# Attention and hash-routed experts on one core: transposes a pair ahead of the scores, row-table sums behind the outputs, warm-up ahead of the routing sums

## The chip, the cores and the metric

The kernel runs on one core of one Trainium2 chip. Its time is device microseconds, the median of three runs; the profile is one further execution of the same program. PE is TensorE (PEld its weight loads), DVE VectorE, ACT ScalarE, POOL GpSimd, SP SyncE.

## The reference

Two stages are joined. The first is causal attention in blocks of 64 over 8 sequences of 576 positions, 8 heads of 64. The second sends every one of the 4608 resulting rows to one of 8 experts, chosen by a hash of its token id, and applies two matrix products with a ReLU between them.

```python
scores = scale * np.matmul(q, k.transpose(0, 1, 3, 2))     # B, H, S, D = 8, 8, 576, 64
scores = np.where(block_i >= block_j, scores, -1000000000.0)
attn = softmax(scores)
x = np.matmul(attn, v)                                      # to rows of 512: N = B * S = 4608
...
expert_idx = token_ids * np.int64(2654435761) % np.int64(E) # E = 8
out[mask] = np.maximum(x[mask] @ w1[e], 0.0) @ w2[e]        # D = 512, F = 1024
```

## The kernel before

Everything is placed by hand: every engine runs its instructions in the order in which the program writes them, and only semaphores order the engines among themselves. A place in the program text is therefore a place in five queues.

**Attention.** The work is cut into 32 pairs of heads, `g` = 0 to 31, four pairs for each sequence `b`. The main loop has one turn for each pair, and a last turn, g = 32, for what is left. In a turn:

- `S_chunk(g, 0)` and `S_chunk(g, 1)`: PE makes two of three chunks of scores (L172, with the mask matmuls at L182) into a PSUM tile `ps` of pool `psS` (two buffers). ACT takes the exponential of each into `pt` (L200).
- In some turns `place_b`: five matmuls on PE (L412) that add a share of the row table, and a DVE addition into `acc` (L415). They use the last 144 columns of the first bank of the tile `O` (pool `psO`, one buffer), which `place_b` allocates; `PV` of the same turn then uses the tile's first 325 columns.
- `PV(g - 1, m)`: the outputs of the pair before (L237, L242), into `O`.
- `norm(g - 1)`: DVE divides by the row sums and writes `xs` (L254, L255).
- `S_chunk(g, 2)`: the third chunk, and at the first pair of a sequence `S_rest`, the last 64 positions (L208, L213).
- `T_group(b, n)`: one of four groups of 18 transposes of a later sequence (L159) into `tp` (pool `psT`, one buffer), which DVE copies to `qT` or `kT` (L164). Groups 2 and 3 are the keys, 0 and 1 the queries. Before the change sequence b's four groups lie in turns 4b-4 to 4b-1, and its scores begin in turn 4b.
- `steps`: pieces of the routing. `route` is a generator that computes, for every token, its slot among the experts; its scan (L304) and the count sums on PE (L318, L319) belong to turn 0. `place_a` makes one-hot tables on DVE (L387, L391), `place_p` multiplies them on POOL (L398, L401), and `place_b` sums them, four turns after `place_a`. The turns of `place_b` are 9, 11, ... 23 (`mids`). `placed` turns the sums into the row table `perm3` in turn 24.
- `write_x`: once a sequence is finished, its rows go to `x_dram` (L263, L265), on SP's queue for sequences 0 to 4, on POOL's for 5 to 7.
- `loads`: POOL issues the inputs of later sequences (`load_qk` L107, `load_v` L124 and L127) and the first experts' weights (`load_w1` L449, `load_w2` L454). Inputs are cast from float32 to bfloat16 on the way.
- `gather_x(e, t0, t1)`: indirect reads of rows of `x_dram` for an expert (L461). The first three blocks of experts 0 and 1 need only sequences 0 to 5, and are issued in turns 26 and 27.

Ahead of the loop come the constants, the first part of `route` (five small matmuls at L286 which wait for the token ids on DVE), the loads of sequences 0 and 1, 40 matmuls on a tile of ones (`warm`, L478), and the four transpose groups of sequence 0, whose copies are shared between DVE and ACT.

**Experts.** After the loop POOL gathers the remaining rows. For each expert PE transposes the gathered rows (L553), DVE copies them to `xT` (L554), PE makes the hidden layer (L566, L585), ACT the ReLU (L571, L589), PE the output (L599), DVE copies it (L604) and POOL scatters it to the result (L606). The tiles `xT` lie where attention's buffers were.

Of the kernel before, what the change touches and what calls it, by code (L numbers as in the profile page):

```python
# [10 lines left out]
F32 = mybir.dt.float32  # L11
# [20 lines left out]
GA = EARLY // 128  # L32
OVT = 32
NG = E * G + OVT
WARM = 40
# [5 lines left out]
def kernel(  # L41
# [10 lines left out]
    nc = tc.nc  # L52
    P = nc.NUM_PARTITIONS
# [13 lines left out]
    onesbf = const.tile([P, P], BF16, name="onesbf")  # L67
# [4 lines left out]
    ov_i = const.tile([1, OVT + 1], I32, name="ov_i")  # L72
    inc = const.tile([P, E], F32, name="inc")

    nc.gpsimd.iota(jmp[:], pattern=[[1, P]], base=0, channel_multiplier=-1,
                   allow_small_or_imprecise_dtypes=True)
    nc.vector.tensor_single_scalar(identbf[:], jmp[:], 0.0, op=ALU.is_equal)
    nc.vector.tensor_single_scalar(lower[:], jmp[:], 0.0, op=ALU.is_gt)
    nc.vector.memset(onesbf[:], 1.0)

    nc.vector.memset(maskk[:], 0.0)
    nc.vector.memset(maskq[:], 0.0)
# [5 lines left out]
    psS = att_ctx.enter_context(tc.tile_pool(name="psS", bufs=2, space=bass.MemoryType.PSUM))  # L88
    psT = att_ctx.enter_context(tc.tile_pool(name="psT", bufs=1, space=bass.MemoryType.PSUM))
    psO = att_ctx.enter_context(tc.tile_pool(name="psO", bufs=1, space=bass.MemoryType.PSUM))  # L90
# [30 lines left out]
    def load_v(b):  # L121
        vx, v4 = vexts[b % NV]
        for i in range(NT):
            nc.gpsimd.dma_start(  # L124
                vx[:, :, i, 0:D], v[b, :, 128 * i : 128 * i + 128, :].rearrange("h p d -> p h d"))
        for m in range(2):
            nc.gpsimd.dma_start(  # L127
                v4[64 * m : 64 * m + 64, :, m, 0:D],
                v[b, 4 * m : 4 * m + 4, 512:576, :].rearrange("r s d -> s r d"))
# [20 lines left out]
    def T_group(b, n, pool=None):  # L150
        if b not in qkTs:
            qkTs[b] = [att.tile([P, NP, S], BF16, name=x, tag=x, bufs=3) for x in ("qT", "kT")]
        w, z = divmod(n, 2)
        c0, n = RUN // 2 * z, RUN // 2
        pool, tag = pool or (psT, "tp")
        tp = pool.tile([P, 16, P], BF16, name="tp", tag=tag)
        for c in range(n):
            for m in range(2):
                nc.tensor.transpose(out=tp[64 * m : 64 * m + 64, c, :],  # L159
                                    in_=loaded[b][w][:, m, c0 + c, :], identity=identbf[:])  # L160
        parts = ((nc.vector.tensor_copy, 0, P),) if b > 0 else (
            (nc.vector.tensor_copy, 0, 64), (nc.scalar.copy, 64, P))
        for copy, r0, r1 in parts:
            copy(qkTs[b][w][:].rearrange("p r (j c) -> p (r j) c", c=RUN)[:, r0:r1, c0 : c0 + n],  # L164
                 tp[:, 0:n, r0:r1].rearrange("p c r -> p r c"))
# [25 lines left out]
    def S_chunk(g, ch):  # L191
        b, pr = divmod(g, NP)
        ps = psS.tile([P, 2, 512], F32, name="ps", tag="ps")
        for n, (o0, kt, q0, w) in enumerate(CHUNKS[ch]):
            mm_pair(b, pr, ps, o0, kt, q0, w, first=n == 0)
        for o0 in MASKS[ch]:
            mm_mask(ps, o0, last=o0 == MASKS[ch][-1])
        pt = pts[g % 2]
        ptv = pt[:, 0 : 2 * PTW].rearrange("p (m n) -> p m n", m=2)
        nc.scalar.activation(ptv[:, :, 512 * ch : 512 * ch + 512], ps[:], ACT.Exp, scale=SCALE)  # L200
# [24 lines left out]
    ots = {}  # L225

    def PV(g, m):
        b, pr = divmod(g, NP)
        h = pr + NP * m
        pt = pts[g % 2]  # L230
        vx, v4 = vexts[b % NV]
        if g not in ots:
            ots[g] = psO.tile([P, 2, 512], F32, name="O", tag="O")
        O = ots[g][:, m, 0 : 5 * (D + 1)].rearrange("p (t d) -> p t d", t=5)
        for t in range(5):
            for n, (o0, i) in enumerate(PVS[t]):
                nc.tensor.matmul(  # L237
                    O[:, t, :], lhsT=pt[:, m * PTW + o0 : m * PTW + o0 + 128], rhs=vx[:, h, i, 0 : D + 1],
                    start=(n == 0), stop=(n == t),
                )  # L240
            if t == 4:
                nc.tensor.matmul(  # L242
                    O[:, t, :], lhsT=pt4s[b % 2][:, pr * 64 : pr * 64 + 128],
                    rhs=v4[:, pr, m, 0 : D + 1], start=False, stop=True,
                )

    def norm(g):
        b, pr = divmod(g, NP)
        if b not in xss:
            xss[b] = xfix[b % 3]  # L250
        xs = xss[b]
        O = ots.pop(g)[:, :, 0 : 5 * (D + 1)].rearrange("p m (t d) -> p m t d", t=5)
        rs = att.tile([P, 2, 5, 1], F32, name="rs", tag="rs")
        nc.vector.reciprocal(rs[:], O[:, :, :, D : D + 1])  # L254
        nc.vector.tensor_tensor(  # L255
            out=xs[:].rearrange("p t (m r d) -> p r m t d", m=2, r=NP)[:, pr],
            in0=O[:, :, :, 0:D], in1=rs[:].to_broadcast([P, 2, 5, D]), op=ALU.mult,
        )

    def write_x(b):  # L260
        xs = xss[b]
        eng = nc.sync if b < BA - 1 else nc.gpsimd
        eng.dma_start(  # L263
            x_dram[S * b : S * b + 512, :].rearrange("(t p) d -> p t d", p=P), xs[:, 0:NT, :])
        eng.dma_start(x_dram[S * b + 512 : S * b + S, :], xs[0:64, NT, :])  # L265
# [139 lines left out]

    def place_b(b, g):
        ohp, ohg, _ = places.pop(b)
        ots[g] = psO.tile([P, 2, 512], F32, name="O", tag="O")
        pq = ots[g][:, 0, 512 - 2 * NG :]
        for i in range(5):  # L410
            n = P if i < NT else 64
            nc.tensor.matmul(pq, lhsT=ohp[0:n, i, :],  # L412
                             rhs=ohg[0:n, i, :, :].rearrange("p w g -> p (w g)"),
                             start=(i == 0), stop=(i == 4))
        nc.vector.tensor_tensor(out=acc[:].rearrange("p w g -> p (w g)"),  # L415
                                in0=acc[:].rearrange("p w g -> p (w g)"), in1=pq, op=ALU.add)

# [39 lines left out]
    def gather_x(e, t0=0, t1=G):  # L457
        n = N if t1 > GA else BA * S
        for t in range(t0, t1):
            g = e * G + t  # L460
            nc.gpsimd.indirect_dma_start(  # L461
                out=xgs[g % (2 * G)][:], out_offset=None, in_=x_dram[0:n, :],
                in_offset=bass.IndirectOffsetOnAxis(ap=perm3[:, g : g + 1], axis=0),
                bounds_check=n - 1, oob_is_err=False,
            )


    NPAIRS = B * NP
    nc.sync.dma_start(tid[:], moe_token_ids.rearrange("(b s) -> b s", b=B))
    rgen = route()  # L470
    next(rgen)
    load_qk(0)
    load_v(0)
    load_qk(1)
    load_v(1)
    warm = psS.tile([P, 2, 512], F32, name="warm", tag="ps")
    for n in range(WARM):
        nc.tensor.matmul(warm[:, 0, 0:P], lhsT=onesbf[:], rhs=onesbf[:], start=True, stop=True)  # L478
    T_group(0, 2)
    T_group(0, 3, pool=(psO, "O"))  # L480
    T_group(0, 0, pool=(psS, "ps"))
    T_group(0, 1, pool=(psS, "ps"))

    Ts = {g: [] for g in range(NPAIRS + 1)}
    for b in range(1, B):
        for z, n in enumerate((2, 3, 0, 1)):
            Ts[4 * b - 4 + z].append((b, n))
    steps = {g: [] for g in range(NPAIRS + 1)}
    steps[0] += [lambda: next(rgen), lambda: next(rgen)]
    steps[1].append(lambda: next(rgen))  # L490
# [2 lines left out]
    mids = {}  # L493
# [3 lines left out]
        mids[9 + 2 * j] = j  # L497
    steps[24].append(placed)
    loads = {g: [] for g in range(NPAIRS + 1)}
    for b, at in ((2, 0), (3, 4), (4, 7), (5, 10), (6, 13), (7, 16)):  # L500
        loads[at].append((load_qk, b))
        loads[at + 1].append((load_v, b))
    for g, what in ((19, (load_w1, 0)), (20, (load_w1, 1)), (24, (load_w2, 0)), (27, (load_w2, 1))):
        loads[g].append(what)
    for g in range(NPAIRS + 1):
        b, pr = divmod(g, NP)
        live = g < NPAIRS
        if live:
            S_chunk(g, 0)
            S_chunk(g, 1)  # L510
        if g in mids:
            place_b(mids[g], g - 1)
        if g >= 1:
            PV(g - 1, 0)
            PV(g - 1, 1)
            norm(g - 1)
        if live:
            S_chunk(g, 2)
            if pr == 0:
                S_rest(b)  # L520
        for bn in Ts[g]:
            T_group(*bn)
        for step in steps[g]:
            step()
        if pr == 0 and b >= 1:
            write_x(b - 1)
        if 12 <= g < 12 + 2 * G:
            nc.gpsimd.memset(xgs[g - 12][:], 0.0)
        if g in (26, 27):
            gather_x(g - 26, 0, GA)  # L530
        for load, n in loads[g]:
            load(n)
    att_ctx.close()
# [115 lines left out]
    with tc.For_i(0, n_ov, 1) as j:  # L649
# [21 lines left out]
        for ft in range(NFT):  # L671
            hp = psY.tile([P, P], F32, name="hpo", tag="yp")
            for db in range(NKT):
                nc.tensor.matmul(hp[:], lhsT=w1b[:, db, ft::NFT], rhs=xt[:, db, :],
                                 start=(db == 0), stop=(db == NKT - 1))
            nc.scalar.activation(ht[:, ft, :], hp[:], ACT.Relu)
        yp = psY.tile([P, DM], F32, name="ypo", tag="yp")
        for ft in range(NFT):
            nc.tensor.matmul(yp[:], lhsT=ht[:, ft, :], rhs=w2b[:, ft, :],
                             start=(ft == 0), stop=(ft == NFT - 1))  # L680
# [36 lines left out]
```

The softmax here doesn't subtract the row's maximum and nothing guards it: scores larger than these inputs give would overflow.

## Time and profile before

| | |
|---|---|
| time, median of three runs | 337.07 us (336.7 to 337.87) |
| span of the profiled execution | 337.6 us |
| PE busy | 263.3 us (78%) |
| POOL busy | 167.9 us (50%) |
| ACT busy | 143.3 us (42%) |
| DVE busy | 138.5 us (41%) |
| first scores (L172) | 14.8 us |
| last `xs` of attention (L255) ends | 149.05 us |
| last scatter (L606) starts | 327.70 us |
| DMA moved | 50.36 MB, 149 GB/s over the span |

Shares of the whole span mix two stages. Attention ends at 149 us, the experts take the rest; what the change does must be read from the first stage and from the hand-over to the second. An engine's idle time counts only where the others wait for it at that moment, so the waits and the order of events at one place matter more than the sums.

### The profile page before, as it was taken

Reading aid. Unit: us, or ns where it says so; the run is one execution under the profiler, and the core shown is the slowest. Engines: PE = TensorE matmul, PEld = TensorE weight load, DVE = VectorE, ACT = ScalarE, POOL = GpSimd, SP = SyncE. Lnnn points to the kernel's source line nnn. Section 1 sums busy time; section 2 is a strip of 40 time slices with the busy share of each in tenths; the row PEclk is TensorE's granted clock in tenths of the full one; section 3 lists DMA queues with packets and bytes.
Section 4 is the critical chain, followed back from the end, with each engine's and each line's share of the span. In section 5 each row is a group of like instructions: output and inputs, shape, how many; then the busy total and the mean of one; then the engine's idle time right before and its main releaser. Section 6 shows DMA issues by size and latency. Waiting matters only on the chain. (4 is left out here: it accounts for less than half of the span.)

```text
span 337.6 us, 7650 instructions
## 1 busy us (share of the span) xinstructions
PE 263.3 (78%) x3255; PEld 195.2 (58%) x3255; DVE 138.5 (41%) x263; ACT 143.3 (42%) x173; POOL 167.9 (50%) x217
## 2 busy tenths in 40 slices
PE   1749768786878765747789899799798897999970
PEld 1637656575756654535576594675666746668430
DVE  6347696777777544321111414033132140330430
ACT  1437768686868655832252060330320503314000
POOL 8838937949950252116237507437257174050550
PEclk9958999999999995896799999999799999999996
DMA  7999699999999098212109979677766786337330
GB/s 104 181 185 171 109 196 227 136 207 186 190 190 228 34 213 165 80 62 59 47 19 209 188 191 221 176 141 220 160 108 229 139 217 179 66 140 127 128 132 12
DMA packets 53571, 50.36 MB, mean 149 GB/s; under 512 B 40098, under 2 KB 44004, under 8 KB 51488
## 3 DMA queue, kind: packets, MB, share of 16 engines
q0 software_dynamic: 50480, 46.87, 78.2%
q1 hardware_dynamic: 3056, 2.99, 2.9%
q8 instruction: 26, 0.43, 0.5%
q14 instruction: 9, 0.07, 0.1%
HBM read 67.15 MB, written 15.20 MB: 244 GB/s over the span
## 5 line engine op out<-in xcount | busy, mean ns | idle before, releaser
L200 ACT ACTIVATE pt<-ps 128x1024 bf16<-128x1024 f32 x96 | 92.6, 1026 | 36.8 <-PE ps L182 33.0
L571 ACT ACTIVATE hT<-hp 128x640 bf16<-128x640 f32 x48 | 33.3, 703 | 95.3 <-PE hp L566 82.5
L599 PE MATMUL yp<-w2b,hT 128*128 128x512 bf16 x320 | 70.2, 379 | 0.0
L566 PE MATMUL hp<-xT,w1b 128*128 128x320 bf16 x384 | 56.2, 304 | 9.0 <-ACT hT L571 6.7
L566 PEld LDWEIGHTS <-w1b 128*128 128x128 bf16 x384 | 52.6, 145 | 12.6 <-issue 10.4
L606 POOL DMA_INDIRECT out_dram<-ysb,perm x40 | 39.8, 994 | 38.8 <-DVE ysb L604 32.2
L461 POOL DMA_INDIRECT xg<-x_dram,perm x40 | 40.5, 1013 | 26.7 <-issue 14.1
L172 PE MATMUL ps<-qT,kT 64*128 64x512 bf16 (+4 forms) x320 | 37.2, 307 | 20.5 <-DVE qT L164 10.2
L599 PEld LDWEIGHTS <-hT 128*128 128x128 bf16 x320 | 31.1, 98 | 36.1
L604 DVE COPY ysb<-yp 128x512 f32<-128x512 f32 x40 | 27.7, 692 | 55.9 <-PE yp L599 47.7
L554 DVE COPY xT<-tpx 128x512 bf16<-128x512 bf16 x40 | 15.5, 420 | 74.2 <-PE tpx L553 68.3
L237 PE MATMUL O<-vx,pt 128*128 128x65 bf16 x896 | 36.1, 197 | 7.8 <-DVE acc L415 3.9
L237 PEld LDWEIGHTS <-pt 128*128 128x128 bf16 x896 | 32.4, 100 | 10.2 <-issue 7.1
L172 PEld LDWEIGHTS <-kT 64*128 64x128 bf16 x320 | 13.3, 95 | 31.3 <-DVE qT L164 12.9
L124 POOL DMA_DIRECT2D vx<-in_v_dram x32 | 28.6, 914 | 0.3 <-issue 0.2
L255 DVE TENSOR_TENSOR xs<-O,rs 128x640 bf16<-128x640 f32 x32 | 26.4, 824 | 1.1
L164 DVE COPY kT<-tp 128x1152 bf16<-128x1152 bf16 (+1 forms) x16 | 20.4, 1283 | 13.5 <-PE tp L159 13.5
L585 PE MATMUL hp<-xT,w1b 128*128 128x384 bf16 (+1 forms) x128 | 21.1, 329 | 3.2 <-DVE xT L554 3.2
L449 POOL DMA_DIRECT2D w1b<-in_moe_w_dram x8 | 4.7, 589 | 35.3 <-PE tpx L553 35.3
L164 DVE COPY qT<-tp 128x1152 bf16<-128x1152 bf16 (+1 forms) x16 | 20.4, 1280 | 3.3 <-PE ps L182 2.6
L589 ACT ACTIVATE hT<-hp 128x768 bf16<-128x768 f32 (+1 forms) x16 | 11.3, 704 | 23.4 <-PE hp L585 11.0
L553 PE MATMUL tpx<-identbf,xg 128*128 128x128 bf16 x160 | 13.7, 220 | 9.1 <-DVE xT L554 7.8
(107 smaller groups left out, 241.3 us busy)
## 6 DMA issues: line engine op xcount, KB each, us to landing
w1b<-in_moe_w_dram POOLq DMA_DIRECT2D x8, 1024.0 KB
w2b<-in_moe_w_dram POOLq DMA_DIRECT2D x8, 1024.0 KB
vx<-in_v_dram POOLq DMA_DIRECT2D x32, 128.0 KB
kb<-in_k_dram POOLq DMA_DIRECT2D x7, 576.0 KB
qb<-in_q_dram POOLq DMA_DIRECT2D x7, 576.0 KB
x_dram<-xs SPq DMA_DIRECT2D x5, 512.0 KB, 8.1
x_dram<-xs POOLq DMA_DIRECT2D x3, 512.0 KB
xg<-x_dram,perm POOLq DMA_INDIRECT x40
```

What stands on the lines that cost most here:

```text
L124: nc.gpsimd.dma_start(vx[:, :, i, 0:D], v[b, :, 128 * i : 128 * i + 128, :].rearrange("h p d -> p h d"))
L164: copy(qkTs[b][w][:].rearrange("p r (j c) -> p (r j) c", c=RUN)[:, r0:r1, c0 : c0 + n], tp[:, 0:n, r0:r1].rearrange("p c r -> p r c"))
L172: nc.tensor.matmul(ps[:, m, o0 : o0 + n], lhsT=kT[rows, pr, 128 * kt : 128 * kt + 128], rhs=qT[rows, pr, q0 : q0 + n], start=first, stop=F ...
L200: nc.scalar.activation(ptv[:, :, 512 * ch : 512 * ch + 512], ps[:], ACT.Exp, scale=SCALE)
L237: nc.tensor.matmul(O[:, t, :], lhsT=pt[:, m * PTW + o0 : m * PTW + o0 + 128], rhs=vx[:, h, i, 0 : D + 1], start=(n == 0), stop=(n == t),)
L255: nc.vector.tensor_tensor(out=xs[:].rearrange("p t (m r d) -> p r m t d", m=2, r=NP)[:, pr], in0=O[:, :, :, 0:D], in1=rs[:].to_broadcast([ ...
L461: nc.gpsimd.indirect_dma_start(out=xgs[g % (2 * G)][:], out_offset=None, in_=x_dram[0:n, :], in_offset=bass.IndirectOffsetOnAxis(ap=perm3[ ...
L566: nc.tensor.matmul(hp[:, t, 0:HC], lhsT=w1b[:, db, ft::NFT], rhs=xT[:, db, t * HC : (t + 1) * HC], start=(db == 0), stop=(db == NKT - 1),)
L571: nc.scalar.activation(hT[:, ft, :].rearrange("p (t n) -> p t n", t=2), hp[:, :, 0:HC], ACT.Relu)
L599: nc.tensor.matmul(yp[:], lhsT=hT[:, ft, tt * P : (tt + 1) * P], rhs=w2b[:, ft, :], start=(ft == 0), stop=(ft == NFT - 1),)
L604: nc.vector.tensor_copy(ysb[:], yp[:])
L606: ins = nc.gpsimd.indirect_dma_start(out=out[:, :], out_offset=bass.IndirectOffsetOnAxis(ap=perm3[:, gg : gg + 1], axis=0), in_=ysb[:], in ...
```

## The change

It has five parts, all in attention.

1. The transposes of a sequence end a pair of heads before its first scores. A turn now has two places for them: place 0 after the second chunk of scores, ahead of `PV`, and place 1 where they were. Sequence 1 has turns 1, 2, 2, 3, sequence 2 has 4, 5, 6, 6, and later sequences 4b-5 to 4b-2.
2. `place_b` comes after `PV` and uses the tile `O` of that `PV`; its addition into `acc` becomes `place_c` and follows `norm` on DVE.
3. The ones are set first of all on DVE, and the warm-up matmuls stand ahead of the routing's first matmuls on PE.
4. Inputs of sequence 2 are issued in turns 1 and 3 instead of 0 and 1; w1 of expert 1 in turn 21 instead of 20, w2 of expert 0 in 22 instead of 24, w2 of expert 1 in 29 instead of 27.
5. The early gathers are issued in turns 28 and 29 instead of 26 and 27.

```diff
+    nc.vector.memset(onesbf[:], 1.0)
     nc.gpsimd.iota(jmp[:], ...)
...
-    nc.vector.memset(onesbf[:], 1.0)
...
     def place_b(b, g):
         ohp, ohg, _ = places.pop(b)
-        ots[g] = psO.tile([P, 2, 512], F32, name="O", tag="O")
         pq = ots[g][:, 0, 512 - 2 * NG :]
...
+        return pq
+
+    def place_c(pq):
         nc.vector.tensor_tensor(out=acc[:].rearrange("p w g -> p (w g)"), ...)
...
+    warm = psS.tile([P, 2, 512], F32, name="warm", tag="ps")
+    for n in range(WARM):
+        nc.tensor.matmul(warm[:, 0, 0:P], lhsT=onesbf[:], rhs=onesbf[:], start=True, stop=True)
     rgen = route()
     next(rgen)
     load_qk(0)
     load_v(0)
     load_qk(1)
     load_v(1)
-    warm = psS.tile([P, 2, 512], F32, name="warm", tag="ps")
-    for n in range(WARM):
-        nc.tensor.matmul(...)
...
-    Ts = {g: [] for g in range(NPAIRS + 1)}
+    Ts = {(g, z): [] for g in range(NPAIRS + 1) for z in range(2)}
     for b in range(1, B):
-        for z, n in enumerate((2, 3, 0, 1)):
-            Ts[4 * b - 4 + z].append((b, n))
+        at = {1: ((1, 1), (2, 0), (2, 1), (3, 0)), 2: ((4, 1), (5, 1), (6, 0), (6, 1))}.get(
+            b, tuple((4 * b - 5 + z, 1) for z in range(4)))
+        for n, gz in zip((2, 3, 0, 1), at):
+            Ts[gz].append((b, n))
...
-    for b, at in ((2, 0), (3, 4), (4, 7), (5, 10), (6, 13), (7, 16)):
-        loads[at].append((load_qk, b))
-        loads[at + 1].append((load_v, b))
-    for g, what in ((19, (load_w1, 0)), (20, (load_w1, 1)), (24, (load_w2, 0)), (27, (load_w2, 1))):
+    for b, g in enumerate((1, 4, 7, 10, 13, 16), 2):
+        loads[g].append((load_qk, b))
+        loads[g + 1 if b > 2 else 3].append((load_v, b))
+    for g, what in ((19, (load_w1, 0)), (21, (load_w1, 1)), (22, (load_w2, 0)), (29, (load_w2, 1))):
...
-        if g in mids:
-            place_b(mids[g], g - 1)
+        for bn in Ts[g, 0]:
+            T_group(*bn)
         if g >= 1:
             PV(g - 1, 0)
             PV(g - 1, 1)
+            if g in mids:
+                pq = place_b(mids[g], g - 1)
             norm(g - 1)
+            if g in mids:
+                place_c(pq)
...
-        for bn in Ts[g]:
+        for bn in Ts[g, 1]:
             T_group(*bn)
...
-        if g in (26, 27):
-            gather_x(g - 26, 0, GA)
+        if g in (28, 29):
+            gather_x(g - 28, 0, GA)
```

More of the change, by code (lines that the diff above doesn't have):

```diff
@@ L475 @@
     load_v(1)
-    warm = psS.tile([P, 2, 512], F32, name="warm", tag="ps")
-    for n in range(WARM):
-        nc.tensor.matmul(warm[:, 0, 0:P], lhsT=onesbf[:], rhs=onesbf[:], start=True, stop=True)
     T_group(0, 2)
```

## The prediction

> **What bounds the kernel now.** I read the page first, then the waits of PE, then busy time by stage, then the timeline of two places. The chain of waits is of no use here: it ends after two pieces, 1.1 us long.
>
> The page's head and slices (each digit is tenths of a slice of 8.44 us):
> ```profile
> span 337.6 us, 7650 instructions
> ...
> PE   1749768786878765747789899799798897999970
> ...
> DVE  6347696777777544321111414033132140330430
> ACT  1437768686868655832252060330320503314000
> ...
> PEclk9958999999999995896799999999799999999996
> DMA  7999699999999098212109979677766786337330
> ```
> The reader sees two halves. Up to about 149 us (17 slices, attention) PE, DVE and ACT are all at 6 to 8 tenths and DMA at 9: four engines nearly balanced, none full, so the time is set by hand-overs. After that PE alone is near full; the diff touches nothing there. Two dips of the clock (slices 3 and 4; 15 to 18) lie in attention.
>
> Who PE waits for (us in total, times, longest):
> ```profile
> PE ps L172 <- DVE qT L164: 10.2, 7, 1.5
> ...
> PE O L237 <- DVE acc L415: 3.9, 8, 0.6
> ...
> PE pb L318 <- DVE cnt L316: 3.0, 1, 3.0
> PE ps L172 <- issue: 2.4, 1, 2.4
> ```
> The first line is one wait of 1.46 us at each of seven sequence starts: the scores need the last transposes, whose copy (L164) is still running. The second is the row-table sum: PV (L237) waits until the sum (L415) has left the same PSUM tile.
>
> One such sequence start in the timeline (start, length, idle before):
> ```profile
> 64.42 1.36 DVE L164 COPY qT<-tp 128x1152 bf16<-128x1152 bf16 x1
> 65.69 0.81 DVE L387 TENSOR_TENSOR ohp<-iota_p,slo 128x640 bf16<-128x640 bf16 x1
> ...
> 65.83 0.39 PE L172 MATMUL ps<-qT,kT 64*128 64x512 bf16 x2 [1.46 <-DVE qT L164]
> ...
> 66.36 2.86 ACT L200 ACTIVATE pt<-ps 128x1024 bf16<-128x1024 f32 x3 [1.48 <-PE ps L182]
> ```
> PE and ACT stand still together, so this wait is on the path. The start of the kernel:
> ```profile
> 18.49 1.17 PE L159 MATMUL tp<-identbf,kb 128*64 128x128 bf16 x18 [0.86 <-DMA kb<-in_k_dram]
> ...
> 19.70 1.36 DVE L164 COPY kT<-tp 128x1152 bf16<-128x1152 bf16 x1 [5.02 <-PE tp L159]
> ...
> 22.69 0.20 PE L318 MATMUL pb<-cnt,lower 128*128 128x16 bf16 x1 [3.04 <-DVE cnt L316]
> ...
> 22.85 0.61 PE L172 MATMUL ps<-qT,kT 64*128 64x512 bf16 x2
> ...
> 23.55 1.94 ACT L200 ACTIVATE pt<-ps 128x1024 bf16<-128x1024 f32 x2 [5.11 <-PE ps L182]
> ```
> PE waits for the second sequence's keys, DVE copies their transposes, only then runs the routing scan, and PE waits for that: ACT is idle 5.11 us, and matmuls afterwards take 0.61 us instead of 0.39.
>
> Busy time of a sequence and of two odd stretches (PE, PEld, DVE, ACT, POOL, clock, DMA, GB/s):
> ```profile
> 49.80:65.80 16.00, 12.46 (x282) 9.93 (x282) 12.17 (x19) 11.86 (x13) 12.28 (x16) 1.00 1.30 181
> ...
> 122.30:132.80 10.50, 4.65 (x70) 3.07 (x66) 4.81 (x6) 4.04 (x4) 5.46 (x6) 0.71 0.78 177
> ...
> 149.10:154.70 5.60, 1.19 (x12) 0.99 (x13) 1.18 (x3) 0.00 (x0) 2.38 (x3) 0.63 0.27 107
> ```
> A sequence takes 16.0 us, and no engine has over 12.5 us of work in it.
>
> [...]a clock of 0.50 around 18 to 27 us after PE's idling, 0.61 against 0.39 us. [...]PV writes columns 0 to 324, the sum reads 368 to 511, and PV still waited 8 times.[...]
>
> **The change part by part.** Start-to-start steps, warm, read off the timeline of pairs without waits (pair 24 on PE: scores 0 at 113.08, PV at 113.68, scores 2 at 114.69, end 115.07): first two scores 0.60, PV 1.01, third score 0.38, transposes 0.64, row-table matmuls 0.52 (L412, 101.52 to 102.04). DVE: norm 1.00 (0.26 + 0.74), copy of transposes 1.27 (64.42 to 65.69), one-hots of place_a 1.18 (58.42 to 59.60), sum 0.30. ACT: 0.92 to 0.98 per exponential, 0.41 for S_rest.
>
> *Warm-up first, the ones set first.* The 40 matmuls (4.0 us) now run at 7.26 to 11.26 and hold the first transposes back until 11.19; they move to about 1.5 to 5.5 us, while PE has nothing to do. Then the transposes follow the inputs. The last half of q has landed by 11.5 us (GpSimd waits for it until 11.54). From there 0.69 (warm) to 1.17 us (cold) of transposes and 0.8 of copy: scores start at 13.0 to 13.5 instead of 14.82. I take 13.5[...]. That cold clock stays through pairs 0 and 1, as it does now for pair 1.
>
> *Transposes of sequence 1 after pair 1 instead of pair 0.* The scan now runs straight after the first copies (2.6 us of DVE from about 13.4), so PE finds the counts ready, and pair 1 starts when ACT frees a buffer: about 17.2 instead of 22.85. Pairs 1 to 3 then hold four transposes and copies through one PSUM buffer: copy 1.27 + transposes 0.65 + gap each, with two norms between. Adding these up pair by pair: pair 2 at 21.6, pair 3 at 25.8, pair 4 when the last copy ends, 29.4 against 34.89. So -5.5. Moving loads of sequence 2 to pairs 1 and 3 is hidden: the queue is busy with sequence 1 until about 24 us, and they are needed from pair 4 on.
>
> *Pairs 4 to 7* hold the four transposes of sequence 2 in three pairs plus one of sequence 3, the last routing steps (1.9 of DVE) and two place_a (2.36). DVE: 4 norms 4.0 + 5 copies 6.4 + 1.9 + 2.4 = 14.7 us, the engine that sets the pace, against 14.96 measured from pair 4 to 8; with two waits for the single transpose buffer I get the norm of pair 7 at 47.4 against 51.57. So the gain falls to -4.2 here.
>
> *Sequences 2 to 4 (pairs 8 to 19).* The boundary wait (1.46) goes: copies end a pair ahead. The row-table wait (0.4 to 0.58, two a sequence) goes from PE; the sum queues on DVE behind the norm, and ahead of the copy, which is 0.3 later. The norm itself must now wait for the five row-table matmuls[...]: +0.52. The new cycle of two pairs is: norm 1.00, sum 0.30, copy 1.27, one-hots 1.18, norm 1.00, PV 1.01 (it needs that norm: one O buffer), row-table matmuls 0.52, about 0.2 of latencies: 6.5 us, 12.9 a sequence. PE (5.8 for two pairs) and ACT (5.5 to 6.3) fit beside it. The norm of pair 8 comes at 50.1 (now 56.14), that of pair 20 at 88.9 (now 103.68): -14.8.
>
> *Pairs 21 to 31.* Without one-hots ACT sets it, 5.9 for two pairs: norm of pair 22 at 94.9 (now 110.66), end of attention (last xs, L255) at 122.5 instead of 149.05, if the stall of 122.3 to 130 is not repeated. In that stall PE, ACT and DVE all start late ("issue", which the profile doesn't explain) while six gathers are issued; pair 27 took 10.53 us where 4.5 was due, and pair 28, at half clock, 4.73 for 3.43: 7.3 us together. The gathers move to pairs 28 and 29, so a stall would come with them: 129.8. I can't tell which from this trace and keep both.
>
> *Hand-over to the experts.* The second w2 is now issued after the gathers, at about 121, right ahead of the last write of x. DVE's first xT copy waits for that write (4.12 us now). 1 MB at about 200 GB/s is 5.2 us in the same queue: without the stall this gives back some 4 us, with it nothing, for the weights are through by then. The wait of the gathers for the write of sequence 5 behind the earlier weights is in the queue at about 111 us, when the gathers are due. Zero on PE's path; at most 2.
>
> Sum: -26.5 + 4 = -22.5 without the stall, -19.3 with it. I take -21.5, nearer to no stall: 315.5 us. The stage after it stays 183 us.
>
> **The rivals.** (a) *Only what the waits list comes back.* 10.2 + 3.9 + 3.0, less about 3 for DVE now at its limit, is -14: 323 us. For it: DVE has 12.17 us of work a sequence, so a copy displaced from the boundary displaces something else. Against: ACT idles about 4 us a sequence. (b) *The transfers set the pace; slower.* A sequence brings 1.77 MB of q, k, v and writes 0.59; at 181 to 205 GB/s that is 11.5 to 13.0 us, as long as the new cycle. If later issues leave gaps in the queue, the transposes wait for keys as at 18.49, PE drops to half clock, and with the late second w2 (+4) the total is 337 + 4 = 341. Against: the queue stood empty from 34 to 37 and from 61 to 63 us, and there is lead: ahead of the keys of sequence 7 lie 15.9 MB (seven sequences of 1.77, five writes of 0.59, the keys 0.59), at 190 GB/s through by 3.5 + 84 = 87.5 us, and their transposes come in pair 23, at about 95; sequences 4 to 6 come out at 5 to 8 us of lead in the same way. (c) *Everything fits*: no stall, weights clear of the last write, warm start: -29, 308 us.
>
> **How the numbers follow.** Forecast 0.62, (a) 0.22, (c) 0.10, (b) 0.06 of which a third ends near no change. Hence faster 0.94, same 0.02, slower 0.04. The range leaves out (b) and ends at 308 below and 326 above, where (a) is 3 us worse.
>
> **What would show it.** The seven waits for qT and the eight for acc gone; scores 0 of pair 1 near 17 us; about 13 us from one sequence start to the next in the middle, with DVE over 90% busy; last xs at 122 to 130. Wrong: waits of L159 for kb or qb in mid-run, a sequence period over 14.5, or a second w2 that delays the xT copy by over 6.

## The result, and the profile after

The changed kernel takes 325.62 us (median of four runs, 325.38 to 326.51) against 337.47 us (336.7 to 340.22) for the kernel before on the same chip: a ratio of 0.964, 95% interval 0.958 to 0.970. It is faster by 11.9 us, where 21.5 were forecast; 325.62 lies just inside the upper end, 326, of the range that the prediction gave. Ratios here and below leave out runs that took over 1.5% more than the fastest of their kernel: one of 389.37 us with the early gathers after the attention, and two with the last write on SyncE's queue.

The head of the page after the change, with slices of 8.09 us:

```profile
span 323.7 us, 7645 instructions
...
PE   6788689898989763557998997996997979999960
...
DVE  6567997888987621211015042142240420421330
ACT  1668689888888884113530510502404204124000
...
PEclk9579999999999997559999999999999997999995
```

Attention now fills some 16.5 slices. PE, DVE and ACT stand mostly at 7 to 9 tenths in it instead of 6 to 8. The dip of the clock around slices 16 to 18 is still there (7, 5 and 5 tenths).

Who PE waits for, in the same columns as before (us in total, times, longest):

```profile
PE ps L172 <- ACT pt L200: 14.2, 27, 4.7
...
PE O L237 <- issue: 1.5, 3, 1.0
```

The seven waits for `qT` at the sequence starts, the eight for `acc` and the wait for the routing counts have left the list. At its head is now a wait for ACT. Up to 121 us it is 1.1 us at most each time; one of 4.7 us lies at 127.9. The last line counts stops of PE for which the profile shows nothing that it waited for ("issue"); they come back below.

The start of the kernel in the timeline (start, length, idle before):

```profile
12.03 0.76 DVE L164 COPY qT<-tp 128x576 bf16<-128x576 bf16 x1 [0.69 <-PE tp L159]
12.70 0.82 DVE L304 TENSOR_TENSOR_SCAN cum<-oh 128x320 f32<-128x320 f32 x1
...
12.84 0.61 PE L172 MATMUL ps<-qT,kT 64*128 64x512 bf16 x2 [0.86 <-DVE qT L164]
...
15.89 0.20 PE L318 MATMUL pb<-cnt,lower 128*128 128x16 bf16 x1
...
16.45 0.61 PE L172 MATMUL ps<-qT,kT 64*128 64x512 bf16 x2 [0.33 <-ACT pt L200]
```

The scan runs straight after the first copies, the counts (L318) go through without a wait, and pair 1 starts at 16.45 instead of 22.85. Its matmuls still take 0.61 us, and the granted clock is 0.50 here (12 to 18 us).

The place near 122 us:

```profile
120.47 0.39 PE L172 MATMUL ps<-qT,kT 64*128 64x448 bf16 x4 [1.07 <-ACT pt L200]
...
124.64 1.00 POOL L463 DMA_INDIRECT xg<-x_dram,perm  x1 [0.30 <-issue]
125.64 0.61 POOL L456 DMA_DIRECT2D w2b<-in_moe_w_dram  x1
126.66 0.22 DVE L254 RECIPROCAL rs<-O 128x10 f32<-128x10 f32 x1 [7.36 <-remote]
126.81 1.94 ACT L200 ACTIVATE pt<-ps 128x1024 bf16<-128x1024 f32 x2 [4.57 <-remote]
```

The standstill that the prediction could not explain came again: DVE and ACT are late by several us for no reason that the trace gives ("remote"), while GpSimd goes on issuing. The last `xs` ends at 134.81 us instead of 149.05, and the first copy to `xT` starts at 140.34 instead of 153.18.

### The profile page after: what moved, and what is told of

It is laid out like the page before. It is cut to its first block, busy times and chain, and to the rows that moved or that the text cites. A ratio compares the mean times of both kernels' runs of the same rounds, so it can differ in the third digit from the quotient of the medians.

```text
span 323.7 us, 7645 instructions
## 1 busy us (share of the span) xinstructions
PE 263.2 (81%) x3255; PEld 196.3 (61%) x3255; DVE 139.0 (43%) x263; ACT 143.9 (44%) x173; POOL 168.0 (52%) x217
## 5 line engine op out<-in xcount | busy, mean ns | idle before, releaser
L574 PEld LDWEIGHTS <-w1b 128*128 128x128 bf16 x384 | 52.6, 145 | 12.8 <-issue 10.7
L612 DVE COPY ysb<-yp 128x512 f32<-128x512 f32 x40 | 27.7, 692 | 55.9 <-PE yp L607 47.6
L172 PE MATMUL ps<-qT,kT 64*128 64x512 bf16 (+4 forms) x320 | 38.7, 306 | 15.6 <-ACT pt L200 14.2
L562 DVE COPY xT<-tpx 128x512 bf16<-128x512 bf16 x40 | 15.5, 421 | 74.4 <-PE tpx L561 67.0
L237 PE MATMUL O<-vx,pt 128*128 128x65 bf16 x896 | 36.8, 198 | 2.6 <-issue 1.5
L172 PEld LDWEIGHTS <-kT 64*128 64x128 bf16 x320 | 14.5, 95 | 26.0 <-issue 17.9
L593 PE MATMUL hp<-xT,w1b 128*128 128x384 bf16 (+1 forms) x128 | 20.1, 319 | 2.3 <-DVE xT L562 2.3
L182 PE MATMUL ps<-maskq,maskk 64*128 64x64 bf16 x256 | 21.4, 193 | 0.3 <-issue 0.3
```

The costliest lines, as they stand in the source:

```text
L172: nc.tensor.matmul(ps[:, m, o0 : o0 + n], lhsT=kT[rows, pr, 128 * kt : 128 * kt + 128], rhs=qT[rows, pr, q0 : q0 + n], start=first, stop=F ...
L182: nc.tensor.matmul(ps[:, m, o0 : o0 + 64], lhsT=maskk[rows, :], rhs=maskq[rows, :], start=False, stop=last,)
L237: nc.tensor.matmul(O[:, t, :], lhsT=pt[:, m * PTW + o0 : m * PTW + o0 + 128], rhs=vx[:, h, i, 0 : D + 1], start=(n == 0), stop=(n == t),)
L574: nc.tensor.matmul(hp[:, t, 0:HC], lhsT=w1b[:, db, ft::NFT], rhs=xT[:, db, t * HC : (t + 1) * HC], start=(db == 0), stop=(db == NKT - 1),)
L612: nc.vector.tensor_copy(ysb[:], yp[:])
```

## The experiments

The twelve runs went to three chips, four to each. All ratios are to the kernel before on the same chip, which took 317.6, 316.8 and 317.8 us there (medians), 20 us less than on the first chip. So only ratios are compared with the first chip, and traces mainly among these three.

### Both kernels once more

No edit.

The kernel before:

> The kernel before once more, for its trace beside the others of this call. Theory (the standstill at 122 us and the half clock after it belong to that one chip): no standstill, last outputs of the attention near 140 us instead of 149, whole time near 317.5 us. Rival (it belongs to the kernels): ACT and VectorE stop at about 122 us for some 5 us here too.

The changed kernel:

> The changed kernel once more, for its time and trace beside the others of this call. From the parts measured so far (transposes alone 0.975 of before, the rest without them 1.007) the theory that parts add up gives a ratio of 0.980 to 0.985 on a chip where the kernel before takes 317.5 us: 311 to 313 us. Rival (the 0.964 of the first comparison holds on every chip): 305 to 307 us.

Measured: before 318.55 us in its one run. Changed: 310.16 us, ratio 0.9775 (0.9735 to 0.9815), a little under the 0.980 to 0.985 that the parts add up to (the interval reaches into it), and clear of the 0.964 of the first chip. Neither trace has the standstill:

| trace | scores 0 of pair 8 | of pair 31 | last `xs` ends | wait of the first `xT` copy | first `xT` copy | span |
|---|---|---|---|---|---|---|
| before, first chip | 49.9 | 142.8 | 149.05 | 4.12 | 153.18 | 337.6 |
| changed, first chip | 44.1 | 122.3 | 134.81 | 5.52 | 140.34 | 323.7 |
| before, again | 50.1 | 135.8 | 141.99 | 5.00 | 146.99 | 316.9 |
| changed, again | 44.6 | 120.4 | 126.65 | 9.93 | 136.58 | 307.9 |

Up to 122 us the kernel before runs alike on both chips (pair 27 starts at 122.3 and 122.6). The other 20.7 us of its span come after: 7.1 up to the last `xs`, and 14.5 in the experts (184.4 against 169.9 us from the first `xT` copy to the end), less 0.9 in the hand-over between them. So the standstill is nothing that either kernel must bring with it; what brought it on that chip stays open.

Without it attention gains 15.3 us, and the hand-over gives 4.9 of them back. The experts, whose code no edit changes, took 1.4 us more in the changed kernel's trace, so 9.0 us of the span remain.

How far two traces agree matters for all that follows. In six traces the code of the attention's turns is the same but for the turns of weight loads and gathers, and yet on the three chips its last `xs` ends between 126.65 and 130.7 us. Most of the spread lies in gaps on PE that the profile gives no releaser for ("issue" in its lists). Their sum in four pairs, beside the time that these pairs took, in us (the runs that the rows name are described below):

| trace | gaps, pairs 12 to 16 | time | gaps, pairs 24 to 28 | time |
|---|---|---|---|---|
| changed, again | 1.02 | 14.14 | none | 11.94 |
| changed, first chip | 0.81 | 14.04 | 0.96 | 12.88 |
| warm-up back | 1.09 | 14.32 | none | 11.97 |
| loads back | 0.50 | 13.73 | 0.28 | 12.24 |
| last w2 earlier | 1.26 | 14.38 | 1.52 | 13.42 |
| gathers late | 1.93 | 15.05 | 1.51 | 13.43 |

The time grows by as much as the gaps: without them it is 13.1 to 13.2 us in every row of the first stretch and 11.9 to 12.0 in every row of the second. The kernel before shows no such gap between pairs 8 and 20. What causes them isn't shown; no run takes them away alone.

### Transposes alone, and everything but the transposes

Transposes alone, in the kernel before:

```diff
-    Ts = {g: [] for g in range(NPAIRS + 1)}
-    for b in range(1, B):
-        for z, n in enumerate((2, 3, 0, 1)):
-            Ts[4 * b - 4 + z].append((b, n))
+    Ts = {(g, z): [] for g in range(NPAIRS + 1) for z in range(2)}
...
+        for bn in Ts[g, 0]:
+            T_group(*bn)
```

> The kernel before with one part of the change: the two places for transposes in a pair, and their new pairs. Theory (waits for qT): the seven waits of 1.46 us ahead of a sequence's first scores go, so the time falls from 337.5 us by 8 to 11 us, to about 328, and the last pair's outputs end near 139 instead of 149. Rival (the output place O is what holds PE, freed by the moved row-table sums): the transposes alone bring under 3 us, to 335 or more.

The reverse of this edit, in the changed kernel:

> The changed kernel with the transposes at their old places. Theory (waits for qT): the waits of about 1.46 us ahead of each first scores are back and most of the 11.9 us gain is lost: 333 to 336 us. Rival (O freed by the moved sums): the gain mostly stays, 326 to 329 us.

Measured: transposes alone 309.22 us, ratio 0.9752 (0.9717 to 0.9787); last `xs` at 131.75, 10.2 us earlier than before. Everything else alone: 319.9 us, ratio 1.0068 (1.0044 to 1.0091); last `xs` at 138.81, 3.2 us earlier. In the second trace PE's waits between 15 and 130 us have the line

```profile
PE ps L172 <- DVE qT L164: 11.4, 7, 1.8
```

The waits for `qT` are back with the old places. So the transposes carry most of the gain in attention, as the theory says, and above all at the start: pair 8 starts at 46.4 us with them alone, at 50.7 without them. In pairs 8 to 20 the two halves gain nearly alike, 4.0 and 3.5 of the 47.6 us before. The rest, which gains 3.2 us by the end of attention, left the whole kernel 0.7% over the kernel before: its first `xT` copy waited 8.65 us for the last write, where the transposes alone left 4.14. So on these chips the transposes alone are worth as much as all five parts (0.9752 and 0.9775, with intervals that overlap): what the others gain in attention, a late write takes back. Where the loads stand, below, is about that write. The new turns for sequence 2's inputs were not tried by themselves.

### The sums behind the outputs

```diff
+            if g in mids:
+                place_c(place_b(mids[g], g - 1))
             PV(g - 1, 0)
             PV(g - 1, 1)
-            if g in mids:
-                pq = place_b(mids[g], g - 1)
             norm(g - 1)
-            if g in mids:
-                place_c(pq)
```

(and `place_b` allocates the tile `O` again)

> The changed kernel with the row-table sums where they were: matmuls ahead of the outputs PV, and the addition ahead of the norm. Theory (PV's waits for the sums, 3.9 us in all, lay on the path): the waits come back and the last outputs of the attention move from 126.7 to 129 to 131 us. Rival (beside the other engines' work they cost nothing, and the norm saves the 0.52 us that it now waits for the sums' matmuls): last outputs at 125.5 to 127.5 us.

Measured: the waits are back:

```profile
PE O L237 <- DVE acc L418: 3.6, 8, 0.6
```

Six of the eight lie in pairs 8 to 20. This trace takes 43.6 us there, and so does that of the transposes alone, which has the sums in the same place; neither has a gap. The six traces of the table, with the sums behind the outputs, take 40.9 to 41.9 in spite of their gaps. So these waits were on the path. The last `xs`, 131.08 against 126.65, does not tell, for traces with the sums behind come as late as 130.7. The whole time, 312.15 us, ratio 0.9796 (0.9741 to 0.9851), overlaps that of the changed kernel.

### The warm-up

The edit moves the 40 warm-up matmuls back behind the loads, and the memset of the ones that they read behind the constants.

> The changed kernel with the warm-up matmuls and the ones they read where they were. Theory (they hold the first transposes back): first scores at 14.8 instead of 13.0 us, and all that follows 1.5 to 2 us later: last outputs of the attention near 128.5, time 1.5 to 2 us over the changed kernel. Rival (the first pairs wait for later inputs and copies, so the start is made up): first scores later, but last outputs within 0.5 us of 126.7.

Measured: first scores at 15.5 us instead of 13.0, pair 8 at 46.7 instead of 44.6, last `xs` at 130.38. The 2.1 us stay at least as far as pair 8, so the start isn't made up for. The further 1.6 us after it are not the edit's: from pair 8 on the gaps on PE add up to 2.97 us here and to 1.36 in the changed kernel. The time, 312.19 us, ratio 0.9805 (0.9737 to 0.9874), overlaps that of the changed kernel.

### The early gathers after the attention

```diff
-        if g in (28, 29):
-            gather_x(g - 28, 0, GA)
+        if g == 32:
+            gather_x(0, 0, GA)
+            gather_x(1, 0, GA)
```

> The changed kernel with the six early gathers issued after the attention's last write instead of in turns 28 and 29. Theory (the standstill of ACT and VectorE from 122.3 to 126.7 us comes from the issue of those gathers): no standstill, the last pair's outputs end near 130 instead of 134.8; the gathers' 7.6 us of issue then follow the last write, so the whole time is 322 to 329 us. Rival (the standstill comes at a time of its own, or from the clock): ACT and VectorE stop near 122.3 us as before, the last pair ends near 134.8, and the time is 328 to 333 us.

Measured: 309.99 us, ratio 0.9751 (0.9709 to 0.9794), last `xs` at 130.7. There was no standstill, but on these chips none came with the early gathers either, so this run decides nothing about it. That the last `xs` comes 4.1 us later than in the changed kernel is again in the main its larger gaps (4.48 us against 1.36 from pair 8 on).

### Where the loads stand

All four turns of weight loads and gathers as before:

```diff
-    for g, what in ((19, (load_w1, 0)), (21, (load_w1, 1)), (22, (load_w2, 0)), (29, (load_w2, 1))):
+    for g, what in ((19, (load_w1, 0)), (20, (load_w1, 1)), (24, (load_w2, 0)), (27, (load_w2, 1))):
...
-        if g in (28, 29):
-            gather_x(g - 28, 0, GA)
+        if g in (26, 27):
+            gather_x(g - 26, 0, GA)
```

> The changed kernel with the turns of the expert weight loads and of the early gathers as before (gathers in turns 26 and 27, the last w2 load in turn 27). Theory (the change's later turns put 1 MB of w2 right ahead of the attention's last write, whose landing took 9.3 us with them and 4.1 us without): the wait of the first xT copy for the last write falls from about 9 to about 4 us, and the time by 3 to 5 us against the changed kernel of this call, to a ratio near 0.97. Rival (the write takes as long whatever is ahead of it, or attention slows by as much): within 1 us of the changed kernel.

Only the last w2 load moved, from turn 29 to 26:

> The changed kernel with one number different: the last w2 load in turn 26 instead of 29, ahead of the gathers; the gathers stay in turns 28 and 29. Theory (it is the w2 load, not the gathers, that holds the last write): the first xT copy waits 4 to 6 us for the write, and the time is 3 to 5 us under the changed kernel of this call. Rival (the gathers hold the write): no gain, within 1 us.

Measured: 305.35 us, ratio 0.9633 (0.9598 to 0.9669), and 306.21 us, ratio 0.9660 (0.9629 to 0.9691): both under the changed kernel's 0.9775, whose interval they don't touch. GpSimd's issues and DVE's first copy, first in the changed kernel on that chip:

```profile
124.32 0.62 POOL L456 DMA_DIRECT2D w2b<-in_moe_w_dram  x1
126.95 0.80 POOL L263 DMA_DIRECT2D x_dram<-xs  x1 [2.00 <-DVE xs L255]
...
136.58 0.76 DVE L562 COPY xT<-tpx 128x512 bf16<-128x512 bf16 x2 [9.93 <-DMA x_dram<-xs]
```

and with the loads back:

```profile
115.39 0.63 POOL L456 DMA_DIRECT2D w2b<-in_moe_w_dram  x1
...
127.40 0.78 POOL L263 DMA_DIRECT2D x_dram<-xs  x1 [10.04 <-DVE xs L255]
...
132.51 0.76 DVE L562 COPY xT<-tpx 128x512 bf16<-128x512 bf16 x2 [5.40 <-DMA x_dram<-xs]
```

The same write, issued at nearly the same time, lands 4 us earlier when 1 MB of weights was issued 12.0 instead of 2.6 us ahead of it. With only that load moved and the gathers in place, the wait is 4.55 us. So it was the weights, not the gathers. On these three chips every run with the last w2 in turn 29, behind the early gathers, waits 8.65 to 9.93 us, and the five others whose copy waits for the write 4.1 to 5.4. The version with the loads back beats both kernels on its chip.

One more step on it, the last write on SyncE's queue:

```diff
-        eng = nc.sync if b < BA - 1 else nc.gpsimd
+        eng = nc.sync if b < BA - 1 or b == B - 1 else nc.gpsimd
```

> The changed kernel with the turns of weight loads and early gathers as before, and also the attention's last write to x issued by SyncE's queue instead of GpSimd's. Theory [...]: the first xT copy waits 3 us or less for the write instead of 5.4, and the time is 2 us under the 305.35 of that kernel. Rival (512 KB takes its 4 us in any queue): within 1 us of 305.35.

Measured: ratio 0.9568 (0.9512 to 0.9624), which overlaps that of the version under it on another chip; in its trace, taken of a run of 310.66 us, its longest, the copy still waits 5.11 us for the write. A gain isn't shown.

### The rest scores

Computed a pair earlier, in the transposes' place:

```diff
-        ps = psS.tile([P, 2, 512], F32, name="ps", tag="ps")
+        ps = (psT.tile([P, 2, 512], F32, name="pr4", tag="tp") if early
+              else psS.tile([P, 2, 512], F32, name="ps", tag="ps"))
...
             S_chunk(g, 1)
+            if pr == NP - 1 and 1 <= b < B - 1:
+                S_rest(b + 1, early=True)
...
-            if pr == 0:
+            if pr == 0 and b < 2:
                 S_rest(b)
```

> The changed kernel with the four heads' rest scores of sequences 2 to 7 computed a pair earlier, in the transposes' PSUM place instead of a ps place. Theory (the rest scores' turn through the two ps places holds the next pair's first scores): the sequence period falls from 13.8 us to 13.0 to 13.4, six times, so attention ends 2.5 to 4.5 us earlier and the time is 321 to 323.5 us. Rival (the period is ACT's and PE's work alone): period and time stay, 325 to 326.5 us. Second rival (the rest scores now hold the transposes in their one place): 326.5 to 329 us.

Measured: 312.5 us, ratio 0.9849 (0.9818 to 0.9881), worse than the changed kernel's 0.9775. The second rival held. At the last pair of a sequence PE now waits for the copy that frees the place, and ACT behind it:

```profile
73.15 0.31 PE L209 MATMUL pr<-qT,kT 64*64 64x64 bf16 x8 [1.19 <-DVE qT L164]
75.27 2.91 ACT L200 ACTIVATE pt<-ps 128x1024 bf16<-128x1024 f32 x3 [1.39 <-PE ps L182]
```

Left out altogether for sequences 2 to 7 (the `if` above without the early call):

> The changed kernel without the rest scores (key tile 4 of the last 64 queries, four matmul pairs and one exponential) of sequences 2 to 7: that part of the computation is left out, to measure it. Theory (their turn through the two ps places costs more than ACT's 0.4 us): the period of sequences 2 to 6 falls from 13.4 to 14.1 us to 12.8 to 13.1, near the 12.9 forecast. Rival (only ACT's 0.4 us or less comes back, and something else makes the period): 13.2 to 13.8 us.

Measured, sequence periods in us (scores 0 to scores 0), from the start of pair 8:

| | 8 to 12 | 12 to 16 | 16 to 20 | 20 to 24 | 24 to 28 |
|---|---|---|---|---|---|
| changed, again | 13.39 | 14.14 | 13.42 | 13.60 | 11.94 |
| without rest scores | 13.14 | 12.64 | 12.64 | 13.51 | 12.16 |
| forecast | 12.9 | 12.9 | 12.9 | 11.9 | 11.8 |

Over the first three the changed kernel takes 40.95 us, without the rest scores 38.42, and 38.7 were forecast. So the period fell as far as the theory said (0.25, 1.50 and 0.78 us), but not for its reason alone: the changed kernel's trace has gaps on PE of 1.02 us in the second stretch and 0.34 in the third, and the trace without the rest scores has none in all three. Where neither side has a gap in these stretches, the rest scores cost 0.25 us (pairs 8 to 12) and 0.51 (pairs 16 to 20, where the trace with the gathers late has no gap and takes 13.15). That is near ACT's 0.38 us of work on them, as the rival has it; the rest of the fall is the absence of the gaps, which no run explains. The whole time was 308.16 us, ratio 0.9685 (0.9634 to 0.9736), which touches the interval of the changed kernel, for a kernel that does less.

The turn through the buffers can be seen at a sequence start of the changed kernel (again):

```profile
88.98 0.38 ACT L213 ACTIVATE pt<-ps 128x256 bf16<-128x256 f32 x1
...
89.13 0.39 PE L172 MATMUL ps<-qT,kT 64*128 64x512 bf16 x2 [0.18 <-ACT pt L200]
...
89.65 1.94 ACT L200 ACTIVATE pt<-ps 128x1024 bf16<-128x1024 f32 x2 [0.29 <-PE ps L182]
```

The rest scores hold one of the two `ps` buffers and chunk 2 the other. The next pair's first scores start as soon as ACT is through with chunk 2, and ACT, done with the rest scores, stands idle 0.29 us until they are there. It is about 0.3 us at every sequence start of this trace but one, where a gap comes on top:

```profile
61.31 0.64 PE L159 MATMUL tp<-identbf,kb 128*64 128x128 bf16 x16 [0.36 <-issue]
...
61.88 0.39 PE L172 MATMUL ps<-qT,kT 64*128 64x512 bf16 x2
...
62.40 3.95 ACT L200 ACTIVATE pt<-ps 128x1024 bf16<-128x1024 f32 x4 [0.60 <-PE ps L182]
```

PE stops in the middle of the transposes ahead of these scores, they start 0.3 us later than the buffer allows, and ACT stands idle 0.60 us. Without the rest scores ACT goes through six exponentials there (59.36 to 65.28) without a pause.

In pairs 20 to 28 leaving them out changed nothing: 25.54 and 25.67 us. The trace without them shows another wait in pair 21:

```profile
87.98 1.28 POOL L127 DMA_DIRECT2D v<-in_v_dram  x2
...
89.24 0.84 POOL L398 TENSOR_TENSOR ohg<-ohs,vhi 128x360 bf16<-128x360 bf16 x1
90.00 0.83 POOL L401 TENSOR_TENSOR ohg<-ohs,vlo 128x360 bf16<-128x360 bf16 x1
...
90.88 0.57 PE L411 MATMUL O<-ohg,ohp 128*128 128x144 bf16 x5 [0.72 <-POOL ohg L401]
91.49 0.22 DVE L254 RECIPROCAL rs<-O 128x10 f32<-128x10 f32 x1 [1.21 <-PE O L411]
```

GpSimd's products for the row table stand behind loads in its queue, so the sums' matmuls, which are now between the outputs and the norm, make PE and DVE wait. In the changed kernel (again) the products come in time, but DVE's one-hots, which run at the same time there (87.2 to 90.1 us), take 1.21 and 1.11 us instead of 0.82 and 0.53, and the products 1.22 and 1.05 instead of 0.80. Both are read from traces; no run took them away.

## Why the prediction was right and where it was wrong

**Right: direction, mechanism and start.** The waits on `qT`, `acc` and the counts are gone, and the two undone edits put back 11.4 and 3.6 us of waits. Pairs 1 to 4 started at 16.45, 20.36, 24.66 and 28.43 (forecast 17.2, 21.6, 25.8, 29.4), the norm of pair 8 at 50.10 (forecast 50.1). Up to there the working holds to 1.3 us; that pair 8 fits to the last digit is luck in part, for pair 4 came 1.0 us early and the pairs after it lost that again. The granted clock stayed at 0.50 until 19.5 us, as forecast. Transfers were no new bound: no transposes waited for keys or queries in mid-run, so rival (b) fell. Rival (a), 323 us, came nearest to the measured time, but not for its reason, VectorE at its limit: on the first chip VectorE works 11.63 of the 13.39 us of pairs 8 to 11 and 11.93 of the 14.03 of the next four (87 and 85%). That is also less than the "over 90%" that the prediction itself looked for. One reading was off: the second dip of the clock before the change fills slices 16 and 17 (126.7 to 136.9 us), not 15 to 18.

**Wrong: the sum, by 10 us on that chip.** The last `xs`, at 134.81, also lies outside the 122 to 130 us that the prediction named. Its terms, in their order there:

- *The cycle of sequences 2 to 4, 12.9 us a sequence, was sized too small.* It measured 13.65 on average (13.39, 14.14, 13.42), and 13.39 to 14.03 on the first chip. Two terms are missing, both put at nothing. One is the gaps on PE, 1.36 us in these three sequences. The other is the rest scores, 0.25 and 0.51 us where it can be told apart: the prediction saw 0.41 us of work on ACT that fit beside the others, and not that ACT idles 0.3 us behind it for the buffer. In the trace that has neither it is 12.8, so what was counted was counted right. What causes the gaps stays open.
- *Pairs 21 to 31, "ACT sets it", 5.9 for two pairs,* came 1.7 us short in pairs 20 to 24 and 0.1 in the next four. Neither the rest scores nor gaps are the cause: 13.60 us without a gap, 13.51 without the rest scores, for 11.9. GpSimd's late products (PE waits 0.72 us for them without the rest scores), and the longer one-hots beside them (1.21 and 1.11 us), fall there; that they are the whole of it isn't shown. Together with the term above the end of attention came at 126.65 instead of 122.5 where there was no standstill, at 134.81 instead of 129.8 where there was.
- *The choice between the two cases.* The prediction stood nearer to no standstill (-21.5 between -22.5 and -19.3), and the standstill came: 2.2 us. The trace before could not tell: the same two kernels ran without it on another chip.
- *The hand-over.* "Gives back some 4 us" without the standstill and nothing with it: measured 4.9 and 1.4. The cause was right: the wait is 9.9 us close behind the weights, 5.4 and 4.55 clear of them. That it is the queue they share with the write is not shown, for no run puts the write on another queue close behind them. With the standstill the write was issued 9.5 us after the weights, and they were through: the DMA engines moved nothing (0 GB/s) from 133 to 135 us. This is the larger part of why the change is worth more on the first chip (0.964) than on the second (0.9775): 3.5 of the 4.9 us that lie between the gains of the traces (13.9 and 9.0). The experts, 1.0 us less there and 1.4 more here, are 2.4 of them without an explanation, and attention, which gains 1.1 less there, goes the other way.

Added up at the start of the experts on the first chip: -21.5 + 2.2 + 5.0 + 1.4 = -12.9, and -12.8 was measured. Behind that, the experts took 1.0 us less in the trace after; and the profiled execution of the kernel before, 339.2 us, lies 1.7 over its median, so the medians differ by only 11.9.

## What to carry to other kernels

When waits between engines are removed, add up the new cycle by buffers as well as by busy time: here a small tile's turn through a double buffer left ACT idle 0.3 us behind 0.38 us of work. Before a trace is compared with another, add up the gaps that no engine explains: here they moved the end of attention by up to 3 us between traces of nearly the same code. Follow every transfer that an edit moves to what is issued behind it at the next stage's start; here one number, the turn of one weight load, was worth about half of what the change gained on its chip (0.0115 of 0.0225). And read the worth of an edit stage by stage, for a standstill can hide a cost that the edit brings: the hand-over gave back 1.4 us with it and 4.9 without.

## What the runs showed of the hardware

One chip took 20 us more for the same program, with engines late for no reason that the trace names, at about 122 us in both kernels, and with a granted clock of 0.50 from 126.7 to 136.9 us in the kernel before and from 125.3 to past 145 in the changed one, while attention still ran; the traces of three other chips show no such standstill. Of the 20.7 us, 14.5 lay in the experts, which neither kernel changes.

More half clock went with less time than its length here. The versions with the loads back and with the last w2 earlier are the same up to pair 8. Their mean granted clock, and the start of pair 8 in us:

| trace | 0 to 13 us | 13 to 20 | 20 to 30 | 30 to 45 | pair 8 |
|---|---|---|---|---|---|
| loads back | 0.86 | 0.53 | 1.00 | 1.00 | 44.2 |
| last w2 earlier | 0.82 | 0.50 | 0.90 | 0.89 | 46.2 |

If the clock was either 0.50 or 1.00, these means make some 10 and 17 us of half clock (an estimate), so about 7 us more of it went with 2.0 us of time. The record of the clock and the lengths of the matmuls do not always agree, though: with the sums where they were the record is 1.00 up to 45 us, and the first scores of pairs 0 and 1 (at 13.36 and 16.96 us) took 0.61 us all the same.

PE stopped for 0.2 to 1.2 us at a time with nothing that the profile shows to wait for, and each such gap went with about as much time lost in these pairs (the table of six traces).
